# Re-planned order for a chunked attention and gated MLP kernel: PSUM reads of ScalarE and VectorE kept apart in the plan

## The chip, the core and the metric

One core of one Trainium2 chip runs the whole kernel. The metric is the device time of one execution in microseconds; the profile shows one execution with the engines PE (TensorE; PEld are its weight loads), DVE (VectorE), ACT (ScalarE), POOL (GpSimd) and SP (SyncE, which issues the DMAs).

## What is computed

The input has 8 batches of 576 tokens, 8 heads of 64. Attention works inside chunks of 64 tokens, and its output x (576 x 512 for each batch) goes through a gated MLP:

```
scores = (q_c @ k_c.T) / 8;  attn = softmax(scores);  x = attn @ v_c
h = gelu_tanh(x @ w_in)                 # 512 -> 1024
u, v = h[:, :512], h[:, 512:]
v_n = (v - mean(v)) / sqrt(var(v) + 1e-6) * g_ln
v_s = w_sg @ v_n + b_sg[:, None]        # 576 x 576 over the tokens
out = x + (u * v_s) @ w_out             # 512 -> 512
```

The weights w_in and w_out come as 64-bit words, and each float operand is split into a high and a low part, so a product is three matmuls.

## The kernel before

**Tiles.** The 4608 tokens make 36 attention tiles of 128 (tile t holds two chunks of all heads). Batch b needs the tiles whose tokens it owns. The first five tiles (`PE_TILES`) are transposed on PE, through a two-bank PSUM tile named `banks`; the later ones with a DVE transposition and five ACT copies. All other PSUM results sit in the four buffers of `pm`, each two banks wide.

**Start.** `START` lists the steps of batches 0 and 1 by hand, a letter and a number each. L loads a quarter of the v half of w_in; A loads q and k of tiles up to that number, B the v of them; S, T and O are scores with softmax, transposition and attention output of one tile, P and Q the same for two tiles. W and w convert one quarter of the v half of w_in (tiles `wsg`, `wout` before they get their real content, `win_h`, `win_l`), X and x a part of the u half. M and G load the small constants and w_sg, g splits w_sg. v, u, s and o with two digits are units of the MLP of batch 0 or 1. Y converts w_out, V and Z build sums of weight blocks (`w_sums`), E is `odd_diff`, J is `x_sums` for batch 2. From batch 2 on (`FAST`) the products use a seven-product scheme on 2 x 2 blocks; it needs the block sums.

**Later batches.** For b = 2 to 7 the units are v (0 to 3, for even b ahead of them one for the odd columns), u (0 to 4), s (0 to 3), o (0 to 3). `SLOTS[b]` says behind which unit each attention step of the coming pair of batches is called ("10:S9A" calls the scores of two tiles behind unit 10), and `SUMS` where the sums of w_out blocks are called in batch 2.

**Planner.** Nothing of this runs directly. `Recorder` turns each call into an `Op` with a cost (`price`) and dependences; `Plan.due` gives each a due time, walking back from the PE order, less `EARLY` (in thousands of ns, by step; a larger number is due earlier); `Plan.run` simulates the five queues and picks, for every engine but PE, the op with the earliest due time among those that can begin within 200 ns of the first; PE takes its list in order but may reach some 10 us ahead. The instructions are emitted in the order of the simulated starts; each engine then runs its own instructions in that order. SP is one such queue: until step V0 (`IN_ORDER`) its DMAs are taken in program order as far as their tiles are free. So a step that is moved changes the due times and the order in which buffers rotate, not only its own place.

**Around a PSUM result.** `keep` reads one attention output three times: ACT copies it to `xh`, DVE subtracts to get `xl`, ACT copies it to `xf`. The last two don't depend on each other by data; the plan before lets them run at once. `att_scores` reads scores twice on DVE; `first_scores` reads the third tile on DVE and then eight times on ACT.

Of the kernel before, what the change touches and what calls it, by code (L numbers as in the profile page):

```python
# [21 lines left out]
PSUM = bass.MemoryType.PSUM  # L22
# [3 lines left out]
P = 128  # L26
# [19 lines left out]


START = """
L0 A1 S0 L2 L1 A0 S1 L3 B1 A2 W3 W1 A3 T0 S2 W2 B0 T1 W0 w0 O1 A4 w2 X0 O0 T2 M0 w1 S3 w3 v00 O2 T3 S4 G0 O3 v01 T4
A8 x0 O4 X1 B8 v02 x1 v03 X2 g0 g2 v04 g3 U1 U0 X3 x3 x2 P5 g1 F0 F1 u03 P7 g4 u02 s00 s02 s01 Y4 T5 T6 T7 Q5 T8 s03  # L50
Q7 v10 v12 v11 Y0 Y1 Y3 v13 Y5 u10 Y7 u11 Y2 Y6 s10 A11 u12 u13 s11 V0 P9 V1 T9 S13 s12 B10 A10 o01 V2 T10 o02 A12
P11 T13 o03 s13 o00 V3 Q9 T11 B11 Z0 T12 O13 B15 Z1 o10 A17 o11 A15 B12 Z2 o13 Q11 E2 o12 J0 J2 P14 J1
"""

SUMS = {(2, 8): "o0", (2, 9): "o1 o2", (2, 11): "o3"}

PE_TILES = 5

# [6 lines left out]


SLOTS = {
# [5 lines left out]
}  # L73


# [13 lines left out]

REST_V, REST_U = "vppp", "pgvg"  # L90
ENGINES = ("tensor", "vector", "scalar", "gpsimd", "sync")
EARLY = {'K*': 0, 'X*': -8, 's03': 1, 'Y0': -2, 'P7': 5, 'v04': -4, 'X0': -1, 'w3': -3, 'W*': 1, 'g4': 5, 'Y7': -2, 'A10': -4, 'O2': 3, 'u03': -3, 'J2': -2, 'G0': 6, 'S3': -1, 'O1': 0, 'U0': -2, 'A17': -1, 'F1': -3, 'Z2': -1, 'A2': -5, 'A12': 5, 'u10': -6, 'V1': -1, 'B12': 4, 'B1': 1, 'g1': 4, 'B11': -2, 'F0': -2, 'u13': 2, 'A0': 3, 'E2': -1, 'X1': 3, 'v13': 1, 'v02': 4, 'v03': -1, 'U1': -2, 'A1': -2, 'L3': -1, 'g3': -1, 'v10': 8, 'P14': -4, 'T11': 4, 'A8': 2, 'T13': -1, 'o01': 4, 'Q7': 5, 'x3': -1, 'u02': -3, 'A3': -1, 'Y3': 0, 'A4': 0, 'w1': 0, 'Q11': -2, 'B10': 1, 'Z1': 4, 'B0': 1, 'g0': -1, 'o11': 4, 'L1': -1, 'w2': -1, 'T5': 2, 'g2': 2, 'x2': -1, 'u12': -2, 'J1': -1, 'W3': -2, 'o10': 2, 'B15': -2}
AHEAD = 10000
SWITCH = 150
IN_ORDER = "V0"
# [1 line left out]
LATE, DMA_LATE = 0, 3000  # L97
# [4 lines left out]
def is_ap(a):  # L102
    return hasattr(a, "rearrange") and hasattr(a, "tensor")
# [33 lines left out]
class Op:  # L137
    def __init__(self, engine, method, args, kwargs):
        self.engine, self.method, self.args, self.kwargs = engine, method, args, kwargs
        outs = [kwargs["out"] if "out" in kwargs else args[0]]  # L140
        ins = [a for a in (*args[("out" not in kwargs):], *kwargs.values()) if is_ap(a)]
        ins = [a for a in ins if a is not kwargs.get("out") and a is not kwargs.get("accum_out")]
        self.outs, self.ins = outs + [a for a in [kwargs.get("accum_out")] if a is not None], ins
        self.deps, self.succ, self.tiles = set(), [], []
        self.table = next((TABLES.get(f, 0) for f in (*args, *kwargs.values()) if isinstance(f, AF)), 0) if engine == "scalar" else 0
        self.locks = self.waits = self.quarter = False
        self.cost, self.lag = self.price()

    def price(self):

        outs, ins = self.outs, self.ins
        n = max(a.free_size() for a in outs[:1] + ins[:2])
        psum = any(a.space == PSUM for a in outs + ins)
        if self.engine == "tensor":
            x = ins[-1]
            n = outs[0].free_size()
            if x.dtype == F32R:
                return 2.5 + 0.45 * n, 190
            if x.dtype == BF16:
                return 4.6 + 0.42 * n, 190  # L160
            if ins[0].ap[0][1] == D:
                self.quarter = True
                return 29.5, 190
            return (109 if self.method == "transpose" else 1.83 * n + 10), 190
        if self.method == "dma_start" and self.engine == "gpsimd":
            return 1200, DMA_LATE + ins[0].size() / 100
        if self.method == "dma_start":
            row = ins[0].ap[-1][1]
            return (420 if row >= P else 620), DMA_LATE + ins[0].size() / row / 16 * (9 + 0.16 * row)
        wide = [a for a in ins if a.free_size() > 1]  # L170
        copies = self.method in ("tensor_copy", "tensor_scalar") and n > 1
        part = outs[0].ap[0][1] < P
        if self.engine == "gpsimd":
            self.waits = self.method == "tensor_tensor"
            self.locks = self.waits and n > 8
            if "pow" in str(self.kwargs.get("op")):
                return 870, 42
            return (300 + 0.5 * n if not self.waits else 100 + (1.76 if self.kwargs["op"] == ALU.mult else 2.27) * n), 42
        if self.engine == "vector":
            if self.method == "memset":  # L180
                return 600, 85
            self.locks = self.waits = not psum and (len(wide) > 1 or copies)
            if n <= 16:
                return (170 if self.method == "reciprocal" else 100 if self.method == "bn_aggr" else 70), 85
            one = len(ins) == 1 and not psum and self.method in ("tensor_copy", "tensor_scalar")
            three = self.method == "scalar_tensor_tensor" and not psum and len(ins) > 2
            return 65 + (0.53 if one else 1.044) * n + 55 * three + 100 * part, 85
        slow = 120 * (len(outs) > 1) + 90 * (len(ins) > 1)
        return (80 if psum else 100) + (0.8 if psum else 0.825) * n + max(slow, 105 * part), 100
# [10 lines left out]
class Plan:  # L200
# [84 lines left out]
    def run(self, users, after, at):  # L285
# [4 lines left out]
        done = [None] * len(ops)  # L290
# [7 lines left out]
        tensor = [k for k, op in enumerate(ops) if op.engine == "tensor"]  # L298
        pe, table, wire, lanes, mode = 0, 0, 0.0, [0.0] * 8, False
        held = {"vector": [0.0, 0.0], "gpsimd": [0.0, 0.0]}  # L300
        open_ = {e: {k for k, op in enumerate(ops) if op.engine == e and not left[k]} for e in ENGINES}

        def begin(k):
            op = ops[k]
            if left[k]:
                return None
            t = ready[k]
            for name in op.tiles:
                if count[name] < len(users[name]):
                    continue  # L310
                key = key_of[name]
                if not slots[key]:
                    return None
                rank = heads[key].index(name)
                if len(slots[key]) <= rank:
                    return None
                t = max(t, sorted(slots[key])[rank] + WAIT.get(op.engine, 33 + LATE))
            t = max(t, free[op.engine])
            if op.engine == "sync":
                t = max(t, lanes[0], late[k] - HORIZON)  # L320
            if op.waits:
                a, b = held["gpsimd" if op.engine == "vector" else "vector"]
                if a <= t < b:
                    t = b
            return t

        for _ in range(len(ops)):
            best = None
            for e in ENGINES:
# [20 lines left out]
                if e == "tensor":  # L350
                    t, k = min(found)
# [3 lines left out]
                t, k = min(  # L355
                    (late[k] + (1300 if ops[k].table not in (0, table) else 0), b, k) for b, k in found if b <= t0 + 200
                )[1:]
                if best is None or t < best[0]:
                    best = (t, k)
            t, k = best  # L360
            op = ops[k]
            e = op.engine
# [17 lines left out]
                    del lanes[0]  # L380
            if op.locks:
                held[e] = [t, t + cost - 1]
            for name in op.tiles:
                if count[name] == len(users[name]):
                    slots[key_of[name]].remove(min(slots[key_of[name]]))
                    heads[key_of[name]].remove(name)
                count[name] -= 1
                gone[name] = max(gone[name], done[k])
                if not count[name]:
                    slots[key_of[name]].append(gone[name])  # L390
# [35 lines left out]
def block_attention_gated_mlp(ctx: ExitStack, tc: tile.TileContext, qkv, w_in, w_out, w_sg, g_ln, b_sg, out):  # L426
# [177 lines left out]
    def w_sums(kind, step):  # L604
# [14 lines left out]
        def store(n, place):  # L619
            before, nc.early = nc.early, 1000 * EARLY.get("K*", 0)  # L620
            for a, c in zip(kept[kind], place):
# [760 lines left out]
    for step in START.split():  # L1382
        nc.early = 1000 * EARLY.get(step, 0)
        nc.start = nc.start and step != IN_ORDER
# [10 lines left out]
    for b in range(FAST, B):  # L1395
# [4 lines left out]
        for i, ((f, k), then) in enumerate(zip(units, slots)):  # L1400
            f(b, k)
            if (b, i) in SUMS:
                for x in SUMS[b, i].split():
                    sooner(w_sums, x[0], int(x[1]))
# [53 lines left out]
```

## Time and profile before

| | |
|---|---|
| time, median of 3 runs | 504.07 us (503.95 to 506.18) |
| the profiled execution, its own time | 505.13 us |
| its span, first to last instruction | 503.3 us |
| PE busy | 474.7 us (94%) |
| DVE busy | 419.0 us (83%) |
| ACT busy | 343.7 us (68%) |
| POOL busy | 143.5 us (29%) |

The span holds all instructions; 1.83 us of the execution lie around it. Busy times are unions over an engine, so overlapping matmuls are not counted twice. All helper calls pass through one line of the planner (L264), so groups are told apart by the names of tiles.

### The profile page before, as it was taken

Reading aid. Unit: us, or ns where it says so; the run is one execution under the profiler, and the core shown is the slowest. Engines: PE = TensorE matmul, PEld = TensorE weight load, DVE = VectorE, ACT = ScalarE, POOL = GpSimd, SP = SyncE. Lnnn points to the kernel's source line nnn. Section 1 sums busy time; section 2 is a strip of 40 time slices with the busy share of each in tenths; the row PEclk is TensorE's granted clock in tenths of the full one; section 3 lists DMA queues with packets and bytes.
Section 4 is the critical chain, followed back from the end, with each engine's and each line's share of the span. In section 5 each row is a group of like instructions: output and inputs, shape, how many; then the busy total and the mean of one; then the engine's idle time right before and its main releaser. Section 6 shows DMA issues by size and latency. Waiting matters only on the chain.

```text
span 503.3 us, 13159 instructions
## 1 busy us (share of the span) xinstructions
PE 474.7 (94%) x5310; PEld 444.0 (88%) x5310; DVE 419.0 (83%) x740; ACT 343.7 (68%) x627; POOL 143.5 (29%) x134
## 2 busy tenths in 40 slices
PE   3879999999999799999999999999998999999995
PEld 1557898799988699999998999999998999999995
DVE  8787999899885799798987799798978798588565
ACT  4488789925577498956988398937887498635430
POOL 0002300270458835616210513024221523122100
PEclk9999999999999999999999999999999999999999
DMA  8765210207655770538832784439731754145403
GB/s 336 272 225 162 51 37 9 77 1 225 213 162 169 238 213 21 190 110 263 282 84 96 211 255 133 126 100 305 236 73 77 221 169 134 37 140 182 150 1 94
DMA packets 80797, 76.53 MB, mean 152 GB/s; under 512 B 47068, under 2 KB 60640, under 8 KB 80736
## 3 DMA queue, kind: packets, MB, share of 16 engines
q1 hardware_dynamic: 80464, 75.66, 48.6%
q8 instruction: 42, 0.69, 0.5%
q14 instruction: 19, 0.16, 0.1%
q10 hardware_dynamic: 272, 0.03, 0.0%
HBM read 61.51 MB, written 14.16 MB: 150 GB/s over the span
## 4 chain that ended last, share of the span: by engine, by line
PE 65%; ACT 16%; DVE 12%; DMA 3%; issue 2%; POOL 1%; SPq 0%; ACTq 0%; DVEq 0%; POOLq 0%
PE pm L264 63%; ACT ptT L264 5%; ACT xf L264 2%; PE banks L264 2%; DVE nmax L264 2%; DVE xl L264 2%; ACT xh L264 2%; ACT gh L264 1%; DMA out_dram<-ot 1%; ACT pt L264 1%; DVE ot L264 1%; DVE wsg L264 1%; ACT L264 1%; DMA wx<-kept_v 1%; DVE gl L264 1%
## 5 line engine op out<-in xcount | busy, mean ns | idle before, releaser
L264 PE MATMUL pm<-wsg,v 128*128 128x288 f32 x768 | 110.2, 297 | 0.0
L264 PEld LDWEIGHTS pm<-wsg,v 128*128 128x128 f32 x768 | 104.1, 188 | 0.9
L264 ACT COPY ptT<-blocks 32x256 f32<-32x256 f32 (+1 forms) x140 | 62.6, 447 | 8.8 <-DVE blocks L264 6.4
L264 POOL TENSOR_TENSOR sm<-sm,neg_half 128x1 f32<-128x1 f32 x36 | 28.0, 781 | 114.5 <-DVE sm L264 87.1
L264 PE MATMUL pm<-gh,wout 128*128 128x288 f32 x272 | 55.1, 299 | 0.2 <-ACT gh L264 0.2
L264 DVE TENSOR_TENSOR u<-pm,u 128x576 f32<-128x576 f32 (+1 forms) x50 | 36.0, 724 | 13.1 <-PE pm L264 12.9
L264 PEld LDWEIGHTS pm<-gh,wout 128*128 128x128 f32 x272 | 42.7, 188 | 1.4 <-ACT gh L264 0.7
L264 POOL TENSOR_TENSOR pt<-pt,nmax 128x512 f32<-128x512 f32 x27 | 29.1, 1093 | 47.1 <-DVE nmax L264 42.7
L264 ACT ACT_TABLE_LOAD x28 | 35.9, 1283 | 4.5 <-DVE ut L264 2.5
L264 PE MATMUL pm<-gl,wout 128*128 128x288 f32 x136 | 35.7, 299 | 1.0 <-DVE gl L264 1.0
L264 ACT CAST gh<-u 128x576 fp32r<-128x576 f32 x32 | 21.1, 672 | 20.2 <-DVE u L264 20.0
L264 DVE TENSOR_TENSOR gl<-u,gh 128x576 fp32r<-128x576 f32 x32 | 25.3, 792 | 10.5 <-ACT gh L264 10.5
L264 DVE TENSOR_TENSOR ot<-pm,xf 128x576 f32<-128x576 f32 x32 | 24.0, 752 | 8.3 <-PE pm L264 4.1
L264 POOL TENSOR_TENSOR xs<-xf 128x576 f32<-128x576 f32 x12 | 17.5, 1457 | 46.8 <-ACT xf L264 43.1
L264 POOL TENSOR_TENSOR xs<-xf,xs 128x576 f32<-128x576 f32 x12 | 18.2, 1515 | 41.9 <-DVE tx L264 28.8
L264 ACT CAST tx<-xs 128x576 fp32r<-128x576 f32 x24 | 16.2, 675 | 19.6 <-POOL xs L264 18.2
L264 PE MATMUL pm<-win_l,xh 128*128 128x256 f32 (+1 forms) x80 | 26.8, 335 | 1.5 <-ACT hs L264 1.5
L264 PE MATMUL pm<-xl,win_h 128*128 128x288 f32 x112 | 28.1, 298 | 0.0
L264 PE MATMUL pm<-xh,win_l 128*128 128x288 f32 x112 | 28.1, 298 | 0.0
L264 PE MATMUL pm<-xh,win_h 128*128 128x288 f32 x112 | 27.9, 296 | 0.0
L264 PE MATMUL pm<-win_h,xl 128*128 128x256 f32 (+1 forms) x80 | 26.5, 331 | 0.4 <-DVE xl L264 0.4
L264 DVE TENSOR_TENSOR xl<-pm,xh 128x256 fp32r<-128x256 f32 (+2 forms) x37 | 17.4, 490 | 11.2 <-ACT xf L264 10.0
(185 smaller groups left out, 1319.2 us busy)
## 6 DMA issues: line engine op xcount, KB each, us to landing
qk<-qkv SPq DMA_DIRECT2D x31, 512.0 KB, 4.3
wx<-kept_u SPq DMA_DIRECT2D x36, 256.0 KB, 4.5
out_dram<-ot SPq DMA_DIRECT2D x32, 256.0 KB, 2.4
wx<-kept_v SPq DMA_DIRECT2D x30, 256.0 KB, 4.8
wx<-kept_o SPq DMA_DIRECT2D x30, 256.0 KB, 3.0
av<-qkv SPq DMA_DIRECT2D x116, 64.0 KB, 3.2
wsg<-w_in SPq DMA_DIRECT2D x4, 512.0 KB, 3.7
wout<-w_in SPq DMA_DIRECT2D x4, 512.0 KB, 4.1
```

Source lines behind the costliest of these rows:

```text
L264: getattr(getattr(self.nc, op.engine), op.method)(*op.args, **op.kwargs)
```

## The change

Three things. `Op` lists the PSUM tiles that an ACT or DVE instruction touches, and `Plan.run` lets such an instruction begin no sooner than the end of the last access of the other of these two engines to the same tile. The price of one descriptor of an SP transfer in the plan falls from 9 to 5 ns ahead of its 0.16 ns an element. And `START`, `SUMS`, `SLOTS` and `EARLY` are other lists: the same steps in another order.

```diff
@@ -46,13 +46,13 @@
 
 
 START = """
-L0 A1 S0 L2 L1 A0 S1 L3 B1 A2 W3 W1 A3 T0 S2 W2 B0 T1 W0 w0 O1 A4 w2 X0 O0 T2 M0 w1 S3 w3 v00 O2 T3 S4 G0 O3 v01 T4
-A8 x0 O4 X1 B8 v02 x1 v03 X2 g0 g2 v04 g3 U1 U0 X3 x3 x2 P5 g1 F0 F1 u03 P7 g4 u02 s00 s02 s01 Y4 T5 T6 T7 Q5 T8 s03
-Q7 v10 v12 v11 Y0 Y1 Y3 v13 Y5 u10 Y7 u11 Y2 Y6 s10 A11 u12 u13 s11 V0 P9 V1 T9 S13 s12 B10 A10 o01 V2 T10 o02 A12
-P11 T13 o03 s13 o00 V3 Q9 T11 B11 Z0 T12 O13 B15 Z1 o10 A17 o11 A15 B12 Z2 o13 Q11 E2 o12 J0 J2 P14 J1
+A0 L0 B0 A1 L1 L2 L3 B1 A2 A3 S0 W0 T0 S1 W1 S2 w0 w1 T1 W2 O0 O1 W3 w2 T2 S3 M0 w3 v00 O2 A4 T3 X0 O3 G0 S4 v01 A8
+T4 O4 B8 x0 X1 v02 X2 x1 v03 X3 U1 v04 g0 g1 U0 x3 x2 g4 g2 F0 P5 g3 u03 u02 P7 s00 s02 T5 F1 Y4 s01 T6 Q5 T7 T8 Q7
+Y1 Y3 s03 v10 v12 v11 Y0 v13 Y7 Y2 u10 Y6 u11 s10 u12 A11 u13 Y5 A10 s11 V0 P9 V1 T9 S13 s12 o01 V2 B10 T10 A12 o02
+P11 T13 o03 s13 o00 Q9 T11 A17 B15 V3 B11 O13 Z0 T12 A15 Z1 o10 o11 Z2 o13 Q11 B12 P14 E2 o12 J0 J1 J2
 """
 
-SUMS = {(2, 8): "o0", (2, 9): "o1 o2", (2, 11): "o3"}
+SUMS = {(2, 8): "o0", (2, 9): "o1 o2 o3"}
 
 PE_TILES = 5
 
@@ -65,11 +65,11 @@
 
 
 SLOTS = {
-    2: "10:S9A 0:T5 10:O56 10:T8 12:O78 1:S78 4:T6 8:T7",
-    3: "9:T4 2:T1 2:S4 10:O4 1:T0 12:O23 3:S23 9:O01 8:T2 9:T3 9:S56",
-    4: "10:S9A 10:O56 8:T7 9:T8 2:T6 2:S78 1:T5 12:O78",
-    5: "9:T4 2:T1 10:O4 1:T0 3:S23 9:O01 2:S4 12:O23 8:T2 9:T3 9:S56",
-    6: "12:S9A 2:S78 8:T8 12:O78 10:O56 0:T5 6:T7 1:T6",
+    2: "12:T8 10:S9A 0:T5 10:O56 12:O78 0:S78 3:T6 8:T7",
+    3: "9:T4 2:T1 10:O4 12:O23 3:S23 9:O01 9:S56 2:S4 8:T2 9:T3 1:T0",
+    4: "12:T8 10:S9A 0:T5 10:O56 13:O78 0:S78 4:T6 8:T7",
+    5: "10:T4 2:T1 9:O01 10:O4 1:T0 5:S23 2:S4 12:O23 7:T2 9:T3 10:S56",
+    6: "10:S9A 2:T5 12:T8 10:O56 12:O78 3:T6 0:S78 8:T7",
 }
 
 
@@ -89,7 +89,7 @@
 
 REST_V, REST_U = "vppp", "pgvg"
 ENGINES = ("tensor", "vector", "scalar", "gpsimd", "sync")
-EARLY = {'K*': 0, 'X*': -8, 's03': 1, 'Y0': -2, 'P7': 5, 'v04': -4, 'X0': -1, 'w3': -3, 'W*': 1, 'g4': 5, 'Y7': -2, 'A10': -4, 'O2': 3, 'u03': -3, 'J2': -2, 'G0': 6, 'S3': -1, 'O1': 0, 'U0': -2, 'A17': -1, 'F1': -3, 'Z2': -1, 'A2': -5, 'A12': 5, 'u10': -6, 'V1': -1, 'B12': 4, 'B1': 1, 'g1': 4, 'B11': -2, 'F0': -2, 'u13': 2, 'A0': 3, 'E2': -1, 'X1': 3, 'v13': 1, 'v02': 4, 'v03': -1, 'U1': -2, 'A1': -2, 'L3': -1, 'g3': -1, 'v10': 8, 'P14': -4, 'T11': 4, 'A8': 2, 'T13': -1, 'o01': 4, 'Q7': 5, 'x3': -1, 'u02': -3, 'A3': -1, 'Y3': 0, 'A4': 0, 'w1': 0, 'Q11': -2, 'B10': 1, 'Z1': 4, 'B0': 1, 'g0': -1, 'o11': 4, 'L1': -1, 'w2': -1, 'T5': 2, 'g2': 2, 'x2': -1, 'u12': -2, 'J1': -1, 'W3': -2, 'o10': 2, 'B15': -2}
+EARLY = {'K*': 0, 'X*': -8, 's03': 1, 'Y0': -2, 'P7': 4, 'v04': -4, 'X0': -1, 'w3': -1, 'W*': 1, 'g4': 5, 'Y7': -2, 'A10': -4, 'u03': -3, 'J2': -3, 'U0': -2, 'A17': -1, 'F1': -3, 'Z2': -1, 'A12': 9, 'u10': -6, 'V1': -1, 'B12': 8, 'g1': 4, 'B11': -2, 'F0': -2, 'u13': 6, 'E2': -5, 'v13': 1, 'g3': -1, 'v10': 8, 'P14': -4, 'T11': 5, 'T13': -1, 'o01': 4, 'Q7': 9, 'x3': -1, 'u02': -3, 'Y3': 2, 'Q11': -2, 'B10': 1, 'Z1': 4, 'g0': 0, 'o11': 5, 'T5': 2, 'g2': 2, 'x2': -1, 'u12': -3, 'J1': 1, 'o10': 2, 'B15': -2, 'V0': 3, 'O13': 1, 'o12': -4, 'Z0': -8, 'A11': -5, 'o13': -4}
 AHEAD = 10000
 SWITCH = 150
 IN_ORDER = "V0"
@@ -144,6 +144,8 @@
         self.deps, self.succ, self.tiles = set(), [], []
         self.table = next((TABLES.get(f, 0) for f in (*args, *kwargs.values()) if isinstance(f, AF)), 0) if engine == "scalar" else 0
         self.locks = self.waits = self.quarter = False
+        reads = self.ins if engine in ("vector", "scalar") else []
+        self.banks = [a.tensor.name for a in self.outs[: len(reads)] + reads if a.space == PSUM]
         self.cost, self.lag = self.price()
 
     def price(self):
@@ -166,7 +168,7 @@
             return 1200, DMA_LATE + ins[0].size() / 100
         if self.method == "dma_start":
             row = ins[0].ap[-1][1]
-            return (420 if row >= P else 620), DMA_LATE + ins[0].size() / row / 16 * (9 + 0.16 * row)
+            return (420 if row >= P else 620), DMA_LATE + ins[0].size() / row / 16 * (5 + 0.16 * row)
         wide = [a for a in ins if a.free_size() > 1]
         copies = self.method in ("tensor_copy", "tensor_scalar") and n > 1
         part = outs[0].ap[0][1] < P
@@ -298,6 +300,7 @@
         tensor = [k for k, op in enumerate(ops) if op.engine == "tensor"]
         pe, table, wire, lanes, mode = 0, 0, 0.0, [0.0] * 8, False
         held = {"vector": [0.0, 0.0], "gpsimd": [0.0, 0.0]}
+        read = {}
         open_ = {e: {k for k, op in enumerate(ops) if op.engine == e and not left[k]} for e in ENGINES}
 
         def begin(k):
@@ -315,6 +318,8 @@
                 if len(slots[key]) <= rank:
                     return None
                 t = max(t, sorted(slots[key])[rank] + WAIT.get(op.engine, 33 + LATE))
+            for b in op.banks:
+                t = max(t, read.get((b, op.engine == "scalar"), 0.0) + 33 + LATE)
             t = max(t, free[op.engine])
             if op.engine == "sync":
                 t = max(t, lanes[0], late[k] - HORIZON)
@@ -380,6 +385,8 @@
                     del lanes[0]
             if op.locks:
                 held[e] = [t, t + cost - 1]
+            for b in op.banks:
+                read[b, e == "vector"] = done[k]
             for name in op.tiles:
                 if count[name] == len(users[name]):
                     slots[key_of[name]].remove(min(slots[key_of[name]]))
```

## Rows read from the trace of the kernel before

**Rows 1.** Busy time by stage (windows): us, then each engine's busy us with instructions.
```profile
5.71:22.00 16.29, 11.81 (x114) 7.00 (x114) 13.29 (x27) 7.66 (x14) 1.04 (x1) 1.00 0.93 353
22.00:46.00 24.00, 20.60 (x284) 14.60 (x284) 19.02 (x42) 19.42 (x48) 4.13 (x4) 1.00 0.61 189
46.00:150.00 104.00, 103.17 (x1105) 94.93 (x1104) 96.45 (x184) 73.87 (x135) 28.66 (x25) 1.00 0.33 100
150.00:182.00 32.00, 26.45 (x374) 24.07 (x373) 22.36 (x36) 21.61 (x47) 25.87 (x22) 1.00 0.66 202
182.00:498.00 316.00, 312.52 (x3439) 303.39 (x3437) 262.23 (x444) 218.54 (x381) 83.09 (x78) 1.00 0.49 149
498.00:503.30 5.30, 0.14 (x2) 0.00 (x0) 1.96 (x3) 0.00 (x0) 0.00 (x0) 0.90 0.46 135
```

**Rows 2.** Timeline of the first 30 us: start, length, engine, operation [idle before, releaser].
```profile
0.73 0.40 SPq L264 DMA_DIRECT2D wsg<-w_in  x1
...
4.27 0.66 ACT L264 ACTIVATE wsg<-wsg 128x512 f32<-128x512 f32 x1 [1.55 <-DMA wsg<-w_in]
4.96 0.89 DVE L264 TENSOR_SCALAR wsg<-wsg 128x512 f32<-128x512 f32 x2 [0.28 <-ACT wsg L264]
5.71 1.13 PE L264 MATMUL pm<-qk 64*64 64x64 f32 x32 [5.71 <-DMA qk<-qkv]
7.67 0.68 DVE L264 TENSOR_REDUCE nmax<-pm 128x8 f32<-128x512 f32 x1
...
13.45 1.11 PE L264 MATMUL banks<-ident,first_pts 128*128 128x128 f32 x4 [2.91 <-DVE first_pts L264]
14.60 0.59 ACT L264 COPY first_ptT<-banks 128x512 f32<-128x512 f32 x1 [1.34 <-PE banks L264]
15.33 1.09 PE L264 MATMUL banks<-ident,first_pts 128*128 128x128 f32 x4 [0.77 <-ACT first_ptT L264]
...
21.18 0.69 DVE L264 TENSOR_TENSOR xl<-banks,xh 128x512 fp32r<-128x512 f32 x1 [2.55 <-ACT xf L264]
...
26.53 1.13 PE L264 MATMUL pm<-wout,ident 128*128 128x512 f32 x2 [1.44 <-ACT third_pt L264]
28.15 0.47 PE L264 MATMUL pm<-win_h,xl 128*128 128x512 f32 x1
```

**Rows 3.** Busy time by stage (windows) of the start, columns as in Rows 1.
```profile
4.96:13.45 8.49, 4.03 (x68) 2.31 (x68) 8.18 (x18) 4.03 (x7) 0.00 (x0) 1.00 1.02 411
13.45:28.15 14.70, 12.44 (x150) 7.55 (x151) 11.37 (x25) 8.21 (x29) 1.33 (x2) 1.00 0.72 244
28.15:46.00 17.85, 15.94 (x180) 11.74 (x181) 13.47 (x29) 14.84 (x26) 3.84 (x4) 1.00 0.63 196
```

**Rows 4.** Waits over the span: engine, tile <- releaser: us, times, longest.
```profile
DVE xl L264 <- ACT xf L264: 13.9, 17, 2.6
ACT xf L264 <- DVE xl L264: 3.7, 9, 0.5
PE banks L264 <- DVE xl L264: 1.6, 2, 1.2
```

**Rows 5.** The tile `xf`: reads of `banks` on ACT, duration min/median/max, first and last start.
```profile
L264 ACT COPY xf<-banks x7: 372/451/593, 20.6 to 54.5; 128x256 f32<-128x256 f32 x4, 128x512 f32<-128x512 f32 x3
```

**Rows 6.** Timeline around the first units of batch 2.
```profile
169.00 0.50 PE L264 MATMUL pm<-win_h,xodd 128*128 128x512 f32 x1 [2.64 <-ACT win_h L264]
174.03 1.04 POOL L264 TENSOR_TENSOR pt<-pt,nmax 128x512 f32<-128x512 f32 x1
174.10 0.67 ACT L264 CAST tx<-xs 128x576 fp32r<-128x576 f32 x1 [2.09 <-POOL xs L264]
174.79 1.28 ACT L264 ACT_TABLE_LOAD   x1
176.74 0.38 PE L264 MATMUL pm<-win_l,xh 128*128 128x256 f32 x1 [1.45 <-ACT hs L264]
```

**Rows 7.** Matmul groups by shape: count, busy us, mean ns of one, idle before.
```profile
L264 PE MATMUL pm<-wsg,v 128*128 128x288 f32 x768 | 110.2, 297 | 0.0
```

## The prediction

> **What bounds the kernel now.** I read the busy shares first, then the windows that split the span into stages, then PE's waits, then the timeline where PE stands still. PE is busy 474.7 of 503.3 us, so 28.6 us is all that any order can win without taking matmuls away, and the change takes none away. The windows say where these 28.6 us lie [rows 1]: PE starts at 5.71; it idles 16.29 - 11.81 = 4.48 us up to 22 us and 24.00 - 20.60 = 3.40 us up to 46 us; then only 0.83 us up to 150; 5.55 us between 150 and 182, where batch 2 begins; 3.48 us in the 316 us after that; and 5.16 us behind the last matmuls. The sum is 28.61. The reader is to see that from 46 to 150 and from 182 to 498 the kernel is a PE queue with no holes: what is late in the start or at the entrance to batch 2 is pushed through to the end one for one, and there is nearly nothing else to win. The profiled execution took 505.13 us, that is 1.83 around the span, and is 1.06 above the median of 504.07; I take gains off the median.
>
> The tail of 5.16 us is the last block's addition and its store. No list that changes acts on batch 7, so it stays.
>
> **The new rule in the plan.** It makes no instruction wait: the emitted program has these waits already. The DVE subtraction to `xl` stood idle 13.9 us in 17 cases until ACT's copy to `xf` was done, though it needs only `xh`, and ACT's copy stood 3.7 us in 9 cases behind `xl` [rows 4]. One of these is 2.55 us long in the start [rows 2]: DVE's queue had `xl` at its head, and the weight conversion behind it, which was ready, could not pass. The old plan counts this as nothing, so its order is right for a machine that reads PSUM from both engines at once. Planning with the wait, the planner puts one of the two first by due time and fills the other engine's hole with something else. Most of the 13.9 us lie where DVE isn't what PE waits for. What reached PE by this road is 1.6 us, the two waits of transpositions into `banks` for `xl` [rows 4]. So the rule alone is worth about 0 to 1.6 us in the start; I count 0.5 and put the rest on the order.
>
> The rule works by tile name, and `banks` is one name for two banks. The second transposition began at 15.33, 0.14 us after ACT's read of the first half ended (14.60 + 0.59), with 0.77 us of PE idle put down to that copy [rows 2]. That speaks for waits by whole tile in the program too. If it were otherwise, the plan would hold back reads that are free to run: seven `xf` copies from `banks` of 0.45 us median [rows 5], 3.2 us of needless delay planned into ACT and DVE. The Trainium skill bears on this: "PSUM — Partial Sum Buffer", section "PSUM bank collisions raise a hardware error", asks for a guard by bank and quadrant and says that accesses to different banks run clean together. By that rule the copy of one half and the write of the other need no wait, and a plan by tile name is stricter than the chip asks; the sum would then lose up to those 3.2 us. The trace agrees only that there is a wait; it is wider than the page asks for.
>
> **The start, 0 to 46 us.** The old queue is L0, then q and k of tiles 0 and 1; the new one is A0 L0 B0 A1 L1 L2 L3. The first transfer was issued at 0.73 and used at 4.27; the second was used at 5.71 [rows 2]. All have 512 KB here, so they change places: scores of tile 0 can begin near 4.3 us instead of 5.71, and the first conversion near 5.7 instead of 4.27. For PE's first matmul that is -1.4 us, but PE isn't what limits this stage. DVE is: busy 8.18 of the 8.49 us from its first weight op to PE's first transposition [rows 3]. In the new order DVE begins with the maximum over scores, at 4.3 + 1.13 (the scores) + 0.2 = 5.6 instead of 4.96, so it starts 0.65 us late. Against this, the first softmax no longer stands between conversions. From its maximum at 7.67 to its transposition at 13.45 it took 5.78 us with conversion work and the second softmax in between [rows 2]; begun at 5.6 it is through by 11.4 us even so, and sooner if less is put between.
>
> What this is worth at the end of the stage is bounded by DVE's work. Up to the first real product, at 28.15 [rows 2], DVE did 8.18 + 11.37 = 19.55 us in 23.19 us [rows 3]. Begun at 5.6 and packed without a hole it would end at 25.2: at most 3.0 us better. From 28.15 to 46 PE idled 17.85 - 15.94 = 1.91 us more [rows 3], so the stage's bound on the good side is -4.9. On the bad side stand the 0.65 us of DVE's later start and a second copy of the 1.44 us that PE stood behind the eight exponentials of tile 2 [rows 2] (S2 stays the third softmax among the conversions, and with the first two moved forward its ACT chain can meet one more of them): +2.1. I take half of the packed gain, -1.5, and -0.5 from the rule: **-2.0**. The later START steps up to o01 change places too; PE idles only 0.83 us up to 150 [rows 1], which covers them with some 10 us of PE work that may be taken out of order, so 0.
>
> **The entrance to batch 2, 150 to 182 us.** POOL is busy 25.87 of 32 us, DVE 22.36, ACT 21.61 [rows 1]. PE stood 2.64 us until ACT had rewritten a block of `win_h` with a sum that POOL makes (Z2), and 1.45 us until ACT had emptied `pm` through the Gelu, behind a cast that itself waited 2.09 us for POOL and a table load of 1.28 us [rows 6]. The new tail of START calls P14 ahead of E2 and J0 instead of behind them, A17, A15 and B12 elsewhere, and Z0 is due 8 us later. Moving P14 forward adds two POOL products of 1.04 us [rows 6] ahead of E2's differences and of `x_sums`, where tile data of batch 2 are wanted; the loads it triggers are SP's, which isn't short. Good bound: both waits vanish, -4.1. Bad bound: the two products come ahead of Z2's sum and a table load falls between, 2.08 + 1.28 = +3.4. Nothing in the rows decides between them; the longest wait hangs on POOL, and a later Z0 leaves POOL no earlier with Z2. Better-placed casts of x halves speak for a little gain: **-0.8**.
>
> **SUMS and SLOTS.** o1 and o2 stay behind unit 9 of batch 2, and o3 joins them there from behind unit 11, ahead of two s units. A unit is 28 matmuls of 110.2 / 768 = 0.143 us [rows 7], 4.0 us; so its ACT cast and DVE subtraction are called 8 us sooner, and are hidden behind the s units either way. In SLOTS most steps move by one or two units, the largest T8, from behind unit 8, 9 or 10 to 12; T has no PE work, so only its buffers and due times move. The cover is PE's unbroken queue; if it goes, a late transposition costs what it costs today, at most about 0.5 us each time. PE idles 3.48 us in all of 182 to 498 [rows 1]. I take **-0.5**, bounds -2.0 and +2.0. The cheaper descriptors in the plan move due DMAs by 4 ns a descriptor and an engine: 0.
>
> Sum: -2.0 - 0.8 - 0.5 = -3.3, from 505.13 to 501.8 for the profiled execution, from 504.07 to **500.8** for the median. The bounds on either side, -11.0 and +7.5, don't come together; taken as independent they give about -8.5 and +3 around the start.
>
> **Rivals.**
> *Nothing measurable (within 0.5%, 2.5 us).* DVE sets the start and has the same work, begun 0.65 us later; the earlier transposition only moves PE's hole. For it: DVE's 8.18 of 8.49 us. Against: its 3.6 us of holes before 28.15 [rows 3]. Or the rule by tile name holds back the 3.2 us worked out above and eats the -2.0. Time: 503 to 505, say 503.6. Chance 0.27.
> *Slower.* The entrance to batch 2 decides: POOL gets P14's products ahead of Z2's sum, `win_h` comes 2.1 us later and the table load lands in front of the Gelu copy, +3.4; with the start giving nothing this is 507.5. For it: POOL is the fullest helper there. Against: due times should put Z2's sum first. It decides once the `win_h` wait reaches some 5 us. Chance 0.18.
> *Both holes close.* Start -4, entrance -3, rest -0.5: 496.6. For it: these waits are planning errors of the kind the rule mends. Against: DVE is 83% busy. Chance 0.17.
> The forecast itself, 498.5 to 502.5, has 0.38.
>
> **How the numbers follow.** 0.5% is about what a measurement of this kernel can tell from no change; it is 2.5 us, so "faster" is below 501.55. The forecast gives most of its chance there (0.38), the closed holes all (0.17): 0.55 faster, 0.27 same, 0.18 slower. The range runs from 495.5, a little beyond the closed holes, to 506.0, which leaves out the far part of the slower case; the faster cases alone reach from 495.5 to 501.5.
>
> **What would show it right or wrong.** Right: the first scores near 4.3 us, the first transposition at 11.4 or sooner, the first `win_h` product of batch 0 near 26, PE idle of 46 us below 11.6 instead of 13.6; DVE's wait for `xf` far below 13.9 us; PE's wait for `win_h` near 168 no longer than 2.64 us. Wrong: the first real product still at 28 us or later, or PE idle above 6 us at the entrance to batch 2, or new waits between 182 and 498 that sum to more than 5 us.

## Result and the profile after

The changed kernel takes 496.78 us (median of 4 runs, 496.56 to 496.97) against 504.01 us: ratio 0.9848, 95% interval 0.982 to 0.9875. A second measurement on another chip, beside experiments below, gave 0.9826 (0.9796 to 0.9855). The forecast was 500.8 us. It had the sign, and its range of 495.5 to 506 holds the time, but the gain is 7.2 us and not 3.3.

The page of the changed kernel, first lines:

```profile
span 495.0 us, 13167 instructions
## 1 busy us (share of the span) xinstructions
PE 469.8 (95%) x5310; PEld 443.1 (90%) x5310; DVE 419.1 (85%) x740; ACT 343.5 (69%) x627; POOL 149.2 (30%) x134
```

The span is 8.3 us shorter. PE's idle time fell from 28.6 to 25.2 us, only 3.4; PE's *busy* time fell by 4.9 us with the same 5310 matmuls. This is the line that the prediction's first part had no place for.

The stages of the changed kernel (windows, columns as in [rows 1]):

```profile
0.00:4.39 4.39, 0.00 (x0) 0.00 (x0) 2.68 (x7) 1.99 (x4) 0.70 (x6) 1.00 0.58 183
4.39:22.00 17.61, 11.56 (x178) 7.79 (x179) 15.79 (x32) 10.50 (x32) 1.30 (x1) 1.00 1.01 370
22.00:46.00 24.00, 22.06 (x234) 15.46 (x233) 21.75 (x49) 22.73 (x43) 6.53 (x6) 1.00 0.86 232
46.00:150.00 104.00, 103.86 (x1140) 96.52 (x1140) 94.08 (x178) 72.99 (x137) 30.60 (x26) 1.00 0.30 94
150.00:182.00 32.00, 27.34 (x366) 25.51 (x365) 24.53 (x39) 21.57 (x44) 21.98 (x18) 1.00 0.77 226
182.00:489.80 307.80, 305.02 (x3398) 297.79 (x3396) 258.43 (x437) 213.69 (x373) 88.07 (x78) 1.00 0.50 149
```

Up to 46 us PE idles 4.39 + 6.05 + 1.94 = 12.4 us instead of 13.6; between 150 and 182 it is 4.66 instead of 5.55; behind 182 it is 2.78 instead of 3.48. Windows cut at fixed times hold different work in the two kernels, so I also compared the traces at equal work. Each matmul counts as its pitch, the usual time from one start to the next: 0.133 us for 288 columns, 0.235 for 512, 0.1165 for 256, 0.109 for a transposition, and 0.017 for a 64x64 product (a mean, as their starts come in bursts); all of them come to 445.7 us. The table gives the time at which a trace has issued so much work, and how far the changed kernel is ahead. The last column is the second trace of the changed kernel (after_again), from another chip, against the same trace of before. That trace has 5304 of the 5310 matmuls: the records of six 512-column matmuls with `lows`, all before 56 us, are missing, and their 1.4 us of work is counted at their places:

```
work issued   before    after    ahead   ahead, second trace
  40 us        65.29    61.91     3.4      3.1
 120          150.22   146.22     4.0      3.4
 160          198.95   193.85     5.1      4.9
 220          262.16   256.00     6.2      5.8
 240          284.33   276.45     7.9      7.7
 320          366.53   361.40     5.1      5.4
 340          389.48   381.98     7.5      7.8
 445.7 (end)  498.14   489.80     8.3      8.5
```

So the start gave 3.1 to 3.4 us, the stretch up to 150 us 0.3 to 0.6, the entrance to batch 2 1.1 to 1.5, and everything behind it 3.2 to 3.6 us, in steps: +1.7 to +1.9 around 265 to 285, +2.4 around 370 to 390, with 2.3 to 2.8 us given back between them. The execution of the kernel before that was traced took 505.13 us, 1.1 more than its median; that is why the traces are 8.3 us apart and the medians 7.2.

**The start.** Timeline of the changed kernel:

```profile
4.39 1.13 PE L266 MATMUL pm<-qk 64*64 64x64 f32 x32 [4.39 <-DMA qk<-qkv]
5.59 0.69 DVE L266 TENSOR_REDUCE nmax<-pm 128x8 f32<-128x512 f32 x1 [0.92 <-PE pm L266]
11.86 1.09 PE L266 MATMUL banks<-ident,first_pts 128*128 128x128 f32 x4 [2.52 <-ACT first_pts L266]
16.24 1.43 PE L266 MATMUL banks<-first_ptT,av 64*64 64x64 f32 x30 [0.25 <-ACT first_ptT L266]
22.67 0.69 PE L266 MATMUL pm<-qkv_u 64*64 64x64 f32 x32
25.42 0.60 PE L266 MATMUL banks<-ident,third_pt 128*128 128x128 f32 x4
25.77 0.47 PE L266 MATMUL pm<-win_h,xl 128*128 128x512 f32 x1
```

Scores at 4.39, VectorE's maximum over them at 5.59, first transposition at 11.86 instead of 13.45, first real product at 25.77 instead of 28.15: the path that was forecast, the transposition 0.5 us later than the bound given for it.

**The waits.** The groups that answer to [rows 4], of the changed kernel; no wait of `xf` for `xl` is left in its list:

```profile
DVE xl L266 <- ACT xf L266: 2.6, 6, 0.9
PE banks L266 <- DVE xl L266: 1.3, 1, 1.3
```

**The entrance to batch 2.** PE's waits there, and POOL's (timeline of the changed kernel):

```profile
161.85 0.87 PE L266 MATMUL pm<-qk 64*64 64x64 f32 x32 [2.01 <-DMA qk<-qkv]
166.46 0.50 PE L266 MATMUL pm<-win_l,xodd 128*128 128x512 f32 x1 [1.20 <-DVE win_l L266]
167.23 2.80 POOL L266 TENSOR_TENSOR xs<-xf 128x576 f32<-128x576 f32 x2 [3.78 <-DMA out_dram<-ot]
170.70 0.50 PE L266 MATMUL pm<-win_h,tx 128*128 128x256 f32 x2 [0.89 <-DVE tx L266]
```

The 2.64 us for `win_h` are gone, as ACT's cast now comes at 162.66 and not 168.34, but P14's scores stand 2.01 us for their q and k, and POOL's `xs` 3.78 us for a buffer that an output store still holds. One wait took the place of another.

**The place that the forecast missed.** VectorE in the s and o units of batch 3, first in the kernel before:

```profile
256.52 0.65 DVE L264 TENSOR_TENSOR xl<-pm,xh 128x512 fp32r<-128x512 f32 x1
...
259.32 0.42 DVE L264 TENSOR_TENSOR xl<-pm,xh 128x256 fp32r<-128x256 f32 x1 [0.43 <-ACT xf L264]
260.40 0.42 DVE L264 TENSOR_TENSOR xl<-pm,xh 128x256 fp32r<-128x256 f32 x1 [0.65 <-ACT xf L264]
...
274.63 0.75 DVE L264 TENSOR_TENSOR ot<-pm,xf 128x576 f32<-128x576 f32 x1
```

and the same work in the changed kernel:

```profile
250.49 0.65 DVE L266 TENSOR_TENSOR xl<-pm,xh 128x512 fp32r<-128x512 f32 x1
...
252.92 0.69 DVE L266 TENSOR_TENSOR pt<-pm,nmax 128x512 f32<-128x512 f32 x1
253.78 0.76 DVE L266 TENSOR_TENSOR xl<-pm,xh 128x256 fp32r<-128x256 f32 x2 [0.17 <-ACT xf L266]
...
266.75 0.75 DVE L266 TENSOR_TENSOR ot<-pm,xf 128x576 f32<-128x576 f32 x1
```

From the first `xl` to the first `ot` it is 18.11 us before and 16.26 after. ACT's copies of `xf` now follow each other, VectorE does a `pt` subtraction meanwhile and then both `xl` at once. What PE made of it before:

```profile
273.57 0.71 PE L264 MATMUL pm<-gh,wout 128*128 128x288 f32 x2
274.77 0.40 PE L264 MATMUL pm<-gl,wout 128*128 128x288 f32 x1 [0.49 <-DVE gl L264]
...
276.77 0.40 PE L264 MATMUL pm<-gh,wx 128*128 128x288 f32 x1 [0.67 <-DVE ot L264]
```

Two matmuls from 273.57 on take 0.27 us by their pitch, but the next began 1.20 us after the first of them. That is 0.93 us lost, of which the rows show only 0.49 as a hole. The changed kernel passes this place without a wait:

```profile
268.73 0.29 PE L266 MATMUL pm<-gh,wout 128*128 128x288 f32 x1
268.88 0.40 PE L266 MATMUL pm<-gh,wx 128*128 128x288 f32 x1
```

### The profile page after: what moved, and what is told of

It reads as the page before. It is cut to its first block, busy times and chain, and to the rows that moved or that the text cites. A ratio compares the mean times of both kernels' runs of the same rounds, so it can differ in the third digit from the quotient of the medians.

```text
span 495.0 us, 13167 instructions
## 1 busy us (share of the span) xinstructions
PE 469.8 (95%) x5310; PEld 443.1 (90%) x5310; DVE 419.1 (85%) x740; ACT 343.5 (69%) x627; POOL 149.2 (30%) x134
## 4 chain that ended last, share of the span: by engine, by line
PE 72%; DVE 11%; ACT 7%; DMA 5%; issue 1%; SPq 1%; POOL 1%; DVEq 0%; ACTq 0%; POOLq 0%
PE pm L266 71%; DMA out_dram<-ot 2%; ACT ptT L266 2%; DVE u L266 2%; DVE ot L266 2%; DMA wout<-w_in 1%; PE banks L266 1%; DVE sm L266 1%; DVE nmax L266 1%; SPq L266 1%; DVE tx L266 1%; ACT xh L266 1%; DMA qk<-qkv 1%; DVE ts L266 1%; DMA av<-qkv 1%
## 5 line engine op out<-in xcount | busy, mean ns | idle before, releaser
L266 POOL TENSOR_TENSOR sm<-sm,neg_half 128x1 f32<-128x1 f32 x36 | 31.7, 883 | 114.2 <-DVE sm L266 114.0
L266 POOL TENSOR_TENSOR pt<-pt,nmax 128x512 f32<-128x512 f32 x27 | 30.9, 1163 | 51.7 <-DVE nmax L266 47.2
L266 DVE STREAM_TRANSPOSE blocks<-pt 128x512 f32<-128x512 f32 x31 | 21.7, 703 | 9.4 <-POOL pt L266 4.9
L266 PE MATMUL pm<-qk 64*64 64x64 f32 x992 | 20.2, 228 | 9.1 <-DMA qk<-qkv 9.1
L266 PEld LDWEIGHTS pm<-qk 64*64 64x64 f32 x992 | 17.5, 140 | 11.6 <-DMA qk<-qkv 7.3
```

The costliest lines, as they stand in the source:

```text
L266: getattr(getattr(self.nc, op.engine), op.method)(*op.args, **op.kwargs)
```

## Experiments

Theory A: the gain is the planner's knowledge of the wait between ACT's and VectorE's reads. Theory B: it is the order of the lists. Theory C: lists and plan are fitted to each other, and any disturbance of the plan costs. Ratios are to the kernel before on the chip of the run. The expectations call the places around 270, 385 and 442 us the o phases of batches 2, 4 and 6; counted by the products with `wsg` they are those of batches 3, 5 and 6.

**1. Parts by themselves, everything planned anew.**

```diff
 rule_only: before, with
+        self.banks = [...]          # the four edits of the rule, lists and price old
 no_rule: after, without these four edits
 old_slots: after, with SLOTS and SUMS of before
 old_start: after, with START and EARLY of before
```

> The kernel before with the rule for PSUM reads and nothing else; old lists, old descriptor price. If the planner's knowledge of the wait is what gained (theory A), the o phases of batches 2, 4 and 6 lose the DVE waits of xl for xf, DVE's wait for xf falls from 13.9 to under 5 us, and the time is 498 to 501. If the other lists carry the gain (theory B), the waits fall as well but the time stays within 2 us of 504. If old lists were fitted to the old plan and any other plan is worse with them (theory C), it is above 505.

> The changed kernel without the rule for PSUM reads; new lists and new price stay. Theory A: most of the gain goes, 501 to 504, with DVE's wait for xf back near 13 us. Theory B: 496 to 498. Theory C (lists and rule fit each other): above 500, and the loss can exceed what the waits for xf alone explain.

> The changed kernel with the old SLOTS and SUMS: the start as changed, the attention steps and the w_out sums of batches 2 to 6 at their old places. If the 3.3 us that were gained behind 182 us come from the places (theory B), the time is 499 to 501 with the offset to the kernel before at about -5 us from 182 us on. If they come from the rule (theory A), it stays at 496.5 to 498.

> The changed kernel with the old START and EARLY; rule, price, SLOTS and SUMS as changed. If the order of the start is worth the 3.4 us read up to 46 us and the 1.7 us up to 182 us (theory B), the time is 500 to 503. Theory A: 497 to 499, with the start's gain mostly kept, since the rule also repairs the start. Theory C: any value, above 504 possible.

Measured: rule_only 0.9958 (0.9938 to 0.9978); no_rule 1.005 (1.0031 to 1.0069); old_slots 0.9891 (0.9863 to 0.992); old_start 0.9969 (0.9947 to 0.999). Neither A nor B alone stands: the rule with the old lists and price brings 0.4%, the new lists and price without the rule lose 0.5%, and all together win 1.5 to 1.7%. VectorE's wait for `xf` went to 6.6 us with the rule alone, and the steps around 270 and 380 came with it; but 2.9 us were lost at the entrance to batch 2. In no_rule that wait is 6.6 us too, and not near 13. old_slots (499.79 us) met the time of theory B, but not its path: it was 3.0 us ahead at 120 us of work, 1.3 behind the entrance and 4.3 at the end.

**2. Lists held, queues changed.** To switch the rule without moving a step, the plan of a kernel was made as usual, the order of PE, POOL and SP was kept from it instruction for instruction, and VectorE's and ScalarE's queues (in dve_replan VectorE's alone) were planned once more, with or without the rule.

```diff
+        kept = {e: sorted((k for k, op in enumerate(ops) if op.engine == e), key=lambda k: (at[k], k))
+                for e in ENGINES if e not in ("vector", "scalar")}
+        at = self.run(users, after, at, kept)     # engines in kept: the next op of their list, or wait
...
-            for b in op.banks:
+            for b in op.banks if kept is not None else ():   # dve_replan, dve_act_replan (from before)
+            for b in op.banks if kept is None else ():       # blind_dve_act (from after)
```

replan_before has the rule nowhere, replan_after everywhere.

> The kernel before with its own order kept on PE, ACT, POOL and SP, instruction for instruction; only VectorE's queue is planned anew, with the rule. Theory A (the old plan's queue of VectorE is wrong about the wait): the o phases of batches 2, 4 and 6 win most of their 5 us there, time -2 to -4 us against before. Theory B (order of the lists): within 1 us of before, as no step has moved.

> As the run before it, with ScalarE's queue planned anew as well; PE, POOL and SP as in the kernel before. Theory A: as good as or better than VectorE alone, -3 to -5 us, with some of it in the start. Theory B: within 1 us of before.

> The mirror image: the changed kernel with its order kept on PE, POOL and SP, while VectorE's and ScalarE's queues are planned anew without the rule. Theory A: it loses 3 to 6 us against the changed kernel, in the o phases above all. Theory B: within 1 us of the changed kernel (496 to 498).

> The control of the mirror image: the changed kernel, PE, POOL and SP kept, VectorE's and ScalarE's queues planned anew once more with the rule on. Theory A: within 2 us of the changed kernel, so that the 17 us which the same without the rule lost are the rule's. Theory D (a queue that is planned anew behind fixed neighbours is bad by itself): 508 or more, and the mirror image shows little of the rule.

> The control of the other pair: the kernel before, PE, POOL and SP kept, VectorE's and ScalarE's queues planned anew without the rule. Theory A: slower than the same with the rule, so above 509. Theory D: 507 to 510 as with the rule, so the rule makes no difference there.

Measured, against the kernel before: dve_replan 1.0003 (0.9983 to 1.0023), so VectorE's queue alone wins nothing, and A in that form falls. The four with both queues:

| order of PE, POOL, SP from | without the rule | with the rule | with / without |
|---|---|---|---|
| before | 1.0237 (1.0195 to 1.0278) | 1.0055 (1.0032 to 1.0078) | 0.982 |
| after | 1.0185 (1.0148 to 1.0222) | 0.9999 (0.998 to 1.0019) | 0.982 |

Two things follow. With both queues planned once more, the rule is worth 1.8%, some 9 us, behind either order, a difference far outside the intervals. The two runs of each pair ran on two chips, which are exchanged in the second pair. As a plan can move by more than that for other reasons (price_only, below), one pair would show little; that all pairs have the same sign is what counts for A, and 1.8% isn't its size in general: with everything planned anew the rule is worth 0.4% on the old lists and 2.0 to 2.2% on the new ones. And planning two queues once more, under the same rule, costs 2.4% on the kernel before and 1.5 to 1.7% on the changed one: C (and D, as the expectation named it) for what disturbs the fit. replan_after, at 504.87 us, lies between its two expectations. Without the controls the first of these runs read as if the rule did harm. The waits in the four traces, in the table's order:

```profile
DVE xl L268 <- ACT xf L268: 12.4, 15, 2.3
...
ACT xf L268 <- DVE xl L268: 4.2, 10, 0.5
```

```profile
DVE xl L268 <- ACT xf L268: 6.4, 5, 2.6
```

```profile
DVE xl L268 <- ACT xf L268: 10.1, 15, 1.3
...
ACT xf L268 <- DVE xl L268: 4.5, 8, 1.3
```

```profile
DVE xl L268 <- ACT xf L268: 3.2, 5, 1.3
```

With the rule, `xl` waits about 5 times for `xf`, and `xf` not at all for `xl`; without it, 15 times and 8 to 10. At equal work the pair from before differs by 1.9 us at 120, 5.0 at 240, 6.7 at 340 and 7.5 us at the end: mostly behind the entrance to batch 2. The pair from after differs by 2.2, 5.2, 8.3 and 7.9 us.

**3. Where the rule works.** As dve_act_replan, with the rule for one kind of PSUM tile.

```diff
+ ... if a.space == PSUM and "banks" in a.tensor.name]        # replan_banks
+ ... if a.space == PSUM and "banks" not in a.tensor.name]    # replan_pm
```

> The kernel before, PE, POOL and SP kept, VectorE's and ScalarE's queues planned anew with the rule for the tile banks alone (the first five attention tiles). Theory A1 (the rule works where VectorE reads the pm tiles, batches 1 to 6): 513 to 517, as without the rule. Theory A2 (it works in the start, as the prediction had it): 508 to 511, as with the whole rule.

> The same with the rule for every PSUM tile but banks. Theory A1: 507 to 511, as with the whole rule. Theory A2: 513 to 517.

Measured: replan_banks 1.0186 (1.0142 to 1.023), replan_pm 1.0112 (1.0079 to 1.0145), between 1.0237 with neither and 1.0055 with both. The `pm` tiles give 1.25%, clearly; `banks` gives 0.5%, and its interval overlaps that of no rule. So A1 has the larger part. That the rule for `banks` is stricter than needed and costs time, the prediction's second reading, finds no support: it didn't slow this kernel.

**4. The first transfer.** After, with only the first two DMAs of SP's queue exchanged, run twice.

```diff
+        one, two = sorted((k for k, op in enumerate(ops) if op.engine == "sync"), key=lambda k: (at[k], k))[:2]
+        at[one], at[two] = at[two], at[one]
```

> The changed kernel with its first two transfers exchanged on SP's queue (weights, then q and k of tile 0); every other instruction of every engine in its place. If the first scores at 4.4 us are worth their 1.3 us, it loses 1 to 1.5 us. If VectorE's chain absorbs it, it loses under 0.5 us.

> The changed kernel once more, as the base of the three runs beside it. Both theories: ratio to the kernel before within 0.985 +- 0.003.

> The first two transfers exchanged once more, now beside the changed kernel itself. The trace of the first run had the first real product at 27.63 instead of 25.77 us. If PE's unbroken queue pushes this through, it is 1.3 to 2 us slower than the changed kernel; if waits further down absorb it, within 0.5 us.

Measured: swap_first_two 0.9851 (0.9817 to 0.9884); then, side by side, after_again 0.9826 (0.9796 to 0.9855) and swap_again 0.9851 (0.9824 to 0.9877), medians 496.82 and 497.81. The trace of swap_first_two:

```profile
5.59 1.13 PE L268 MATMUL pm<-qk 64*64 64x64 f32 x32 [5.59 <-DMA qk<-qkv]
...
13.05 1.09 PE L268 MATMUL banks<-ident,first_pts 128*128 128x128 f32 x4 [3.78 <-ACT first_pts L268]
...
27.63 0.47 PE L268 MATMUL pm<-win_h,xl 128*128 128x512 f32 x1
```

The transposition comes 1.2 us later and the first real product 1.9. By equal work the two traces with the exchange are 1.9 us behind the changed kernel at 40 us of work, and 1.7 and 1.5 at the end; the medians differ by 1.0 us, between the two expectations. The intervals of the ratios overlap, but all four executions of swap_again (497.45 us and more) are longer than all four of after_again (497.11 and less).

**5. The descriptor price.**

```diff
 price_only: before, with
-            ... (9 + 0.16 * row)
+            ... (5 + 0.16 * row)
 old_price: after, with 9 again
```

> The kernel before with the lower descriptor price in the plan and nothing else. The prediction's 0: within 1 us of before. Theory C (lists fit the plan they were made with, and any other figure undoes the fit): 506 to 511.

> The changed kernel with the old descriptor price. The prediction's 0: within 1 us of the changed kernel, 496 to 498. Theory C: 500 to 506.

Measured: price_only 1.0239 (1.0204 to 1.0273), old_price 1.0012 (0.999 to 1.0035), against 0.9826 to 0.9848 of the changed kernel. A figure that changes 4 ns in the plan, and no instruction by itself, moves the time by 2.4% up on the old lists; taken back on the new ones it loses 1.6 to 1.9%, the whole gain. This is theory C, and the prediction's 0 was wrong as an effect by itself. It also shows that the sum of these waits doesn't set the time by itself. old_price has the rule and about as few of them as the changed kernel (2.6 us), and takes as long as the kernel before:

```profile
DVE xl L266 <- ACT xf L266: 2.7, 6, 0.9
```

**By stage.** The lead over the kernel before at equal work, in us, split into stages by us of work issued (good to some 0.2), for the kernels that were planned anew in whole. The last column is the work that PE issued near the entrance, between 160 and 180 us, while the trace records a granted clock of 0.50:

| run | rule | up to 40 | 40 to 120 | 120 to 160, entrance | behind | work at 0.50 |
|---|---|---|---|---|---|---|
| changed | yes | 3.4 | 0.6 | 1.1 | 3.2 | 0 |
| changed, second trace | yes | 3.1 | 0.3 | 1.5 | 3.6 | 0 |
| rule_only | yes | 1.7 | 0.4 | -2.9 | 2.5 | 2.9 |
| old_slots | yes | 2.7 | 0.3 | -1.7 | 3.0 | 1.9 |
| old_start | yes | -0.9 | 0.6 | -0.4 | 3.2 | 3.2 |
| old_price | yes | 1.0 | 0.2 | -3.5 | 1.7 | 3.3 |
| no_rule | no | 1.5 | 0.5 | -3.6 | -1.5 | 1.8 |
| price_only | no | -1.0 | -0.1 | -5.7 | -7.3 | 2.1 |

Behind the entrance every plan with the rule wins 1.7 to 3.6 us and every plan without it loses. Both steps go with the rule: between 220 and 240 us of work these plans win 1.2 to 1.9 us with it and at most 0.4 without, between 320 and 340 they win 2.0 to 2.5 with it and 0.8 to 1.3 without. The kernel before, the base, has no rule, so rule_only puts the rule at 2.5 us there, and changed against no_rule at 4.7. The places in SLOTS and SUMS matter little there (3.0 of the 3.2 to 3.6 us stay without them). The lead of the start belongs to START and EARLY in the main: without them it is -0.9.

## Why the prediction was wrong

*The sum's premise.* "28.6 us is all that any order can win" failed. It took PE's busy time as work. A 288-column matmul row is 0.297 us long while the next starts 0.133 us after it, so every stall hides some 0.16 us in busy time, and short stalls hide whole. By pitches, the kernel before lost 52.4 us up to its last matmul (498.14 - 445.7) and the changed one 44.1. The Trainium skill, page "Trainium Kernel Development and Optimization", section "Performance Expectations", calls matmul busy time a bad metric for how close a kernel is to roofline, because matmuls are pipelined. The traces agree: of the 8.3 us between them, 4.9 left the busy time and 3.4 the idle time.

*The term of the later batches, -0.5 with bounds of 2.0 either way, is the one that was mis-sized most*: 3.2 to 3.6 us measured, outside its bounds. It was bounded by PE's 3.48 us of idle time behind 182 us and called a queue with no holes. From 150 us of issued work on, the kernel before lost 13.9 us by pitches and the changed one 10.7, while PE's idle time behind 182 us is 3.48 and 2.78.

*The rule was worth "about 0 to 1.6 us in the start; I count 0.5".* The step that failed is "Most of the 13.9 us lie where DVE isn't what PE waits for": those waits did reach PE in the later batches, where the rule is worth 2.5 to 4.7 us in whole plans. With the other queues held it is worth 1.8%, and more than half of that comes from the `pm` tiles. In the start, PE's wait for `xl` at `banks` fell only from 1.6 to 1.3 us.

*The start, -2.0*: 3.4 and 3.1 us in the two traces, by the path forecast, within its bounds. Some of it may be the clock, which the prediction left out: by the section on the hardware, up to an estimated 1.5 us. Two signs of the prediction weren't met, the transposition by 11.4 us (11.86) and an idle time of PE below 11.6 us up to 46 (12.4). *The entrance, -0.8*: 1.1 and 1.5; about right in size, but by exchange: the wait for `win_h` went and one for q and k came. *Up to 150 us, 0*: 0.6 and 0.3. *The combined bounds*: the root of the squares of the single distances gives -7.9 where the prediction has -8.5; the forecast doesn't hang on it.

*The lists as parts with prices of their own.* SLOTS and SUMS taken back lose 2 to 3 us, START and EARLY 6 to 7, the price 8 to 9, the rule 10 to 11; these sum to far more than 7.2. Each also undoes a fit, and by the table by stage much of that loss falls at the entrance to batch 2 (for old_start, in the start). The changed kernel has the rule, and lists and a price that fit it; the kernel before has lists that fit a plan without it. The rival of closed holes gave the right number, 496.6, but not the place. The slower rival's mechanism, P14's products ahead of Z2's sum, didn't occur.

Not settled in whole: why a disturbed plan costs near 2%. One part can be the granted clock. The traces of the kernel before and both of the changed one record no fall of it while PE works, behind their start. Each of the other 15 traces has one near the entrance to batch 2, between 160 and 180 us. In price_only PE was busy 4.18 of the 8 us from 163 to 171, and then the clock fell:

```profile
171.20:177.90 6.70, 4.46 (x15) 3.47 (x15) 5.67 (x8) 4.31 (x7) 3.52 (x3) 0.50 0.66 225
```

At 0.50 its 288-column matmuls start 0.240 us apart instead of 0.133, so work that is issued at 0.50 costs about itself once more, and an estimate of the most that the falls can have cost is the work issued in them: 5.1 us over all three falls of price_only (14.1 us behind the kernel before), 1.7 in replan_before (10.7 behind), 3.6 in replan_after (10.9 behind the changed kernel). So the clock can be a part of the loss and not all of it. Nor does it make the difference between the kernel before and the changed one: executions of the kernel before with a mean granted clock of 0.999 or 1.0 took 504.58 to 505.20 us. The trace of price_only also has longer waits of PE than the kernel before (0.4 us for `xl` and 0.9 for `win_l` there), for example

```profile
PE pm L264 <- DVE xl L264: 3.2, 3, 2.6
...
PE pm L264 <- DVE win_l L264: 2.2, 1, 2.2
```

but no run isolates one of them, and none holds the clock.

## What to carry to other kernels

Where a planner orders the queues, an ordering wait that its model leaves out can cost time even on an engine that seems off the path: here 1.8% with the other queues held, where the waits summed to 10 to 12 us. Judge what PE can still win by start-to-start times against the pitch, not by idle time between rows. And when lists are fitted to a plan, test a rule with the other queues held and with a control that re-plans without it; a part taken back by itself measures the broken fit as well. Compare such runs by stage and at equal work, look for the granted clock in each, and count the matmul records first: six missing ones shift the comparison by 1.4 us.

## What the runs showed of the hardware

In the first 17 to 21 us the same matmuls take longer than later: in the changed kernel 32 score products took 1.13 us at 4.39 and 0.69 at 22.67, and four transpositions 1.09 us at 11.86 and 0.60 at 25.42. The windows' column of the granted clock has 1.00 for both stretches, but the traces' record of the clock begins only at 17.03 us in the changed kernel, 17.82 in its second trace and 20.98 in the kernel before, and the column counts time without a record as 1.00. The trace of dve_replan has a record there, and four transpositions at the pace of the kernel before (1.12 us, and 1.11 at 13.45 in [rows 2]); a window, then the timeline:

```profile
12.40:19.10 6.70, 4.77 (x28) 2.90 (x30) 6.13 (x13) 2.67 (x5) 1.04 (x1) 0.50 0.95 360
13.56 1.12 PE L268 MATMUL banks<-ident,first_pts 128*128 128x128 f32 x4 [3.21 <-DVE first_pts L268]
```

So the slow start fits a grant of 0.50, the lower level of 1.2 GHz; in the other traces this is read from the pace and not from a record. By pitch, the kernel before issued 4.4 us of work ahead of its first record and the changed one 2.9. At half the pace each costs about itself once more, so up to an estimated 1.5 us of the 8.3 between the traces is matmuls that ran at the upper level (2.4 GHz) in the changed kernel and at the lower one before.
